# Block inverses on VectorE in pauses, and one wide matmul for state and output, in an RWKV-7 chunk kernel with a routed expert layer

## The chip, the cores and the metric

The kernel runs on one core of one Trainium2 chip. A core has TensorE (matmul), VectorE, ScalarE and GpSimd, each with its own queue of instructions worked off in order, a sync engine that issues most transfers, and 16 DMA engines. In the profile they are called PE (PEld for its weight loads), DVE, ACT, POOL and SP. The metric is the device time of one execution in microseconds. The kernel before takes 809.48 us, the median of three runs from 804.95 to 816.53.

## The reference

Two layers, the first of which takes most of the time.

```python
# RWKV-7: B, H, S, D = 4, 8, 768, 40; all float32
for t in range(S):
    y[:, :, t] = einsum('bhd,bhde->bhe', rt, state)
    Sa = einsum('bhde,bhe->bhd', state, at)
    state = state * wt[:, :, None, :] - einsum('bhd,bhe->bhde', Sa, bt) \
            + einsum('bhd,bhe->bhde', vt, kt)
# experts: x = y as (3072, 320); E = 8, F = 1024, capacity 80
probs = softmax(x @ w_gate); expert = argmax; gate = probs[expert]
# each expert keeps its 80 tokens of the highest gate:
out[tok] = gate[tok] * (relu(x[tok] @ w1[e]) @ w2[e])   # all other rows are 0
```

The recurrence over 768 steps is worked in chunks of T = 64 steps. Within a chunk the values `U` (the corrections that `a` and `b` make) solve a triangular system with a matrix N of 64x64 per head; it is cut into two diagonal blocks of C = 32, whose inverses are computed beforehand, and one block below the diagonal. There are 12 chunks and 2 pairs of batches: 24 units. The state of a pair of batches passes from unit n to unit n + 2.

## The kernel before

A helper `do` keeps the instructions of every engine in the order in which the parts below are called. `copied` transposes a tile on TensorE (`ps_t` holds the result in PSUM) and copies it to SBUF on ScalarE.

```python
AHEAD = NG + 1                       # NG = 4 units share one round of inverses
ps_t = tile_pool("ps_t", bufs=2, space=PSUM)     # transposes and small products
...
def decays(n):      # transpose w, copy on ScalarE to decay
def products(n):    # pt: scan over decay on VectorE
def decayed_a(n):   # transpose a; ahT = -a * pt on VectorE
def inverted(n):    # pp: pt through TensorE; ip = 1 / pp on VectorE;
                    # ub = b * ip and kh = k * ip on GpSimd

def operands(n):
    of[n]["ubT"] = copied("ubT", pairs(of[n]["ub"]), 1)
    of[n]["khT"] = copied("khT", pairs(of[n]["kh"]), 1)

def system(n):      # both triangles: nt[:, 0] = N from ub, nt[:, 1] from kh
    evicted(nt, scores((ubT, khT), ahT))          # 64 matmuls, one copy on ScalarE
    masked(nt, slice(1, 2))                       # on GpSimd
    # the diagonal blocks of N go to DRAM (blocks)

def begin(k):       # lt = blocks from DRAM, one block per partition
    # mask both 16x16 quarters on the diagonal, set the diagonal to 1
def step(k, i):     # i = 1 .. 14, on both quarters (j = 0, 1) together; n = 15 - i
    nc.vector.tensor_tensor(out=tm, in0=t4[:, :, 0:i, i:i+1].to_broadcast([128, 2, i, n]),
        in1=l4[:, :, i:i+1, i+1:].to_broadcast([128, 2, i, n]), op=mult)
    nc.vector.tensor_tensor(out=t4[:, :, 0:i, i+1:], in0=t4[:, :, 0:i, i+1:], in1=tm, op=add)
def end(k):         # inverses to DRAM (solved), a transposed first quarter too (solved_n);
                    # both come back turned, as dt and an
def joint_n(n):     # na = N's lower quarter times the first inverse: 32 matmuls 16x32 x 32
    nc.scalar.copy(na, p)
def joint(n):       # dn = na times the second inverse: 32 matmuls 32x32 x 16
    nc.vector.tensor_tensor(out=o, in0=p, in1=o, op=add)        # into dt
...
def reads_g(n):     # gT: the state turned, 16 matmuls 64x64 x 64, copied by ScalarE
def right(n):       # pr = masked triangle x v, plus ahT x state_b; yy = pr (ScalarE)
def diagonal(n, i): # u = dt[i] x yy; 16 matmuls 32x32 x 40
    nc.vector.tensor_copy(us[n % 2][:, :, 0:D], o["pr"])
def below(n):       # pr += block below the diagonal x u; yy = pr (ScalarE)

def to_state(n):
    for x, y in ((kh, v), (ub, u)):
        for g, q, z in ...:          # 32 matmuls 64x64 x 40
            nc.tensor.matmul(pg[m, z, g, :], lhsT=x[halves[z], 2*g+q, :], rhs=y[halves[z], 2*g+q, 0:D], ...)
    nc.vector.tensor_tensor(out=acc, in0=pg, in1=st[...], op=add)
    nc.gpsimd.tensor_tensor(out=st[...], in0=acc, in1=pt[last step], op=mult)
    load(n + 2, "v")
def spread(n):      # state_b: two copies of the state by ScalarE

def turned(n):      # uT: u transposed
def lower(n):       # lam = scores of vT and uT against rT, one copy, masked on GpSimd
def rows(n):        # yp = gT x rT
def summed(n):
    for x, l in ((kh, lam 0), (ub, lam 1)):
        for g, q, z in ...:          # 32 matmuls 64x64 x 64
            nc.tensor.matmul(y[m, z, g, :], lhsT=x[halves[z], 2*g+q, :], rhs=lam[halves[z], i, q, g, :], ...)
    # xT = yp * pt on VectorE
def logits(n):      # xp = xT through TensorE; rows to DRAM; logit reduction on VectorE
def gate(ci):       # for 4 units: probabilities, weights (exp on ScalarE between),
                    # candidates (og transposed to gp on TensorE), then 10 x eight (max8, match_replace)
...
for n in range(NU + 1):              # a slot: unit n, the output of o = n - 1, the system of m = n + AHEAD
    operands(m); spread(o)
    # n % 4 == 1: probabilities, weights, candidates; n % 4 == 3: steps 5..14 and end; else: eights
    rows(o); system(m); reads_g(n); right(n); inverted(m + 1); turned(o); diagonal(n, 0)
    lower(o); reads(n, r); reads(n, v); below(n); joint_n(n + 1); decays(m + 2)
    decayed_a(m + 1); diagonal(n, 1); joint(n + 1)
    # n % 4 == 2: begin
    summed(o); to_state(n); products(m + 2)
    # n % 4 == 2: steps 1..4
    logits(o)
```

Before the loop the units 0 to NG are prepared, and the first inverse is computed there. After it come the choice of the 80 tokens of each expert and the experts themselves.

Of the kernel before, what the change touches and what calls it, by code (L numbers as in the profile page):

```python
# [18 lines left out]
def kernel(  # L19
# [116 lines left out]
    with ExitStack() as p1:  # L136

        AHEAD = NG + 1
# [4 lines left out]
        ps_t = p1.enter_context(tc.tile_pool(name="ps_t", bufs=2, space=PSUM))  # L143
# [30 lines left out]
        Q = C // 2  # L174
        QS = Q * C + Q
        (inv_t,) = padded("inv_t", 1, [128, 2 * QS])
        (inv_n,) = padded("inv_n", 1, [128, Q, C])

# [36 lines left out]
        def scores(lhs, rhs):  # L215

            p = ps_s.tile([128, 2, 2, G, T], F32, name="sp", tag="s")
            for i in range(2):
                for g in range(G):
                    for z in halves:  # L220
                        for q, m in enumerate(pars):
                            nc.tensor.matmul(p[z, q, i, g, :], lhsT=lhs[i][m, g, z], rhs=rhs[m, g, z],  # L222
                                             start=True, stop=True)
            return p

        def evicted(o, p):
            nc.scalar.copy(o.rearrange("p i q g t -> p q i (g t)"), p.rearrange("p q i g t -> p q i (g t)"))  # L227

        def masked(o, i):

            for z in halves:
                oo = o[z, i].rearrange("p i q g t -> p (i q g) t")
# [8 lines left out]
        solved_n = nc.dram_tensor("solved_n", (NCI, Z, NS, NG, H, Q * C), F32, kind="Internal")  # L241
# [36 lines left out]
        def operands(n):  # L278
            of[n]["ubT"] = copied("ubT", pairs(of[n]["ub"]), 1)
            of[n]["khT"] = copied("khT", pairs(of[n]["kh"]), 1)  # L280

        def system(n):
            o = of[n]
            o["nt"] = nt = kept.tile([128, 2, 2, G, T], F32, name="nt", tag="nt", bufs=AHEAD + 1)
            evicted(nt, scores((o.pop("ubT"), o.pop("khT")), o["ahT"]))
            masked(nt, slice(1, 2))

            for z in range(Z):
                for i in range(NS):
                    nc.sync.dma_start(blocks[n // NG, z, i, n % NG].rearrange("h (s t) -> s h t", s=C),  # L290
                                      nt[block(z, i), 0].rearrange("p q g t -> p (q g) t")[:, :, i * C : (i + 1) * C])


        def quarters(t):
            return t.rearrange("p (j x) -> p j x", j=2)[:, :, 0 : Q * C].rearrange("p j (s t) -> p j s t", t=C)[:, :, :, 0:Q]

        def fetch(k):
            inverse[k]["lt"] = lt = sb.tile([128, 2 * QS], F32, name="lt", tag="lt", bufs=1)
            nc.sync.dma_start(lt[:, 0 : C * C], blocks[k].rearrange("z i u h x -> (z i u h) x"))

        def begin(k):
            for j in range(2):
                nc.gpsimd.affine_select(out=quarters(inv_t)[:, j], in_=quarters(inverse[k]["lt"])[:, j],
                                        compare_op=Alu.is_gt, fill=0.0, base=0,
                                        pattern=[[-1, Q], [1, Q]], channel_multiplier=0)
            nc.gpsimd.memset(inv_t[:, 0 : C * C : C + 1], 1.0)

        def step(k, i):
            l4, t4 = quarters(inverse[k]["lt"]), quarters(inv_t)
            n = Q - 1 - i  # L310
            tmp = sb.tile([128, Q * Q // 2], F32, name="tmp", tag="tmp", bufs=1)
            tm = tmp[:, 0 : 2 * i * n].rearrange("p (j s t) -> p j s t", j=2, s=i)
            nc.vector.tensor_tensor(
                out=tm, in0=t4[:, :, 0:i, i : i + 1].to_broadcast([128, 2, i, n]),
                in1=l4[:, :, i : i + 1, i + 1 :].to_broadcast([128, 2, i, n]), op=Alu.mult)
            nc.vector.tensor_tensor(out=t4[:, :, 0:i, i + 1 :], in0=t4[:, :, 0:i, i + 1 :], in1=tm, op=Alu.add)
# [548 lines left out]
```

## Time and profile before

| | before |
|---|---|
| median of 3 runs | 809.48 us |
| profiled run, and its span | 807.08 us, 805.3 us |
| mean granted TensorE clock | 0.795 of full speed |
| instructions in the span | 34,678 |
| DMA | 73.00 MB, mean 91 GB/s |
| longest single operations on VectorE: reciprocal, scan | 2,156 ns, 1,232 ns |
| VectorE copies of U | 48, 469 ns each |
| GpSimd masks of `lam` and `nt` | 1,140 ns and 690 ns each |

A line of a group gives the source line, the engine and operation, the tiles (output <- inputs), the shape and the count; after a bar the busy time in us and the mean of one in ns; after another bar the idle time of the engine just before these operations and what ended most of it. A line in order of time begins with the start in us and the duration; square brackets hold the idle time before it and its releaser. "issue" is time in which an engine waited for nothing that the profile shows. One float32 matmul of the source shows as two records (and two weight loads), so the 32 joint matmuls of a unit are 64 records and 24 units give 1,536; a transpose shows as one.

### The profile page before, as it was taken

The page shows a single profiled execution, that of the slowest core. Times are in us where ns is not written, and L with a number is a line of the kernel's source. Part 1 is how long each engine was busy: PE and PEld are TensorE (multiplying, and loading weights), DVE is VectorE, ACT ScalarE, POOL GpSimd, SP SyncE. Part 2 cuts the span into 40 slices and gives each one's busy share as a digit, 9 for nine tenths or more (in the row PEclk, how much of TensorE's full clock was granted, in tenths as well). Part 3 has the DMA queues.
Part 4 walks back from the last instruction along what each step waited for, and adds up shares of the span by engine and source line. Part 5 has one row for each costly group of instructions (what it writes and reads, how often), then busy time and mean ns, then how long its engine had stood idle before and what let it go on. Part 6 is the DMA issues. An engine that isn't in the chain of part 4 may idle for free. (4 is left out here: it accounts for less than half of the span.)

```text
span 805.3 us, 34678 instructions
## 1 busy us (share of the span) xinstructions
PE 601.7 (75%) x15974; PEld 526.9 (65%) x15974; DVE 292.4 (36%) x730; ACT 208.4 (26%) x386; POOL 197.4 (25%) x278
## 2 busy tenths in 40 slices
PE   4750789778786787876989869897878860559997
PEld 3540678667676676765878758787768750458775
DVE  7434223613256242561435624334223218500000
ACT  1320234223442144421444213332213210000010
POOL 4530133222332233321333223322011210020101
PEclk9965787859899797976989768886778865566999
DMA  6556733574245742547323461123411004998000
GB/s 107 93 89 112 76 63 72 131 91 89 56 92 144 91 96 59 112 95 90 57 51 70 117 86 34 31 63 76 52 29 30 13 22 154 353 329 256 17 11 16
DMA packets 238469, 73.00 MB, mean 91 GB/s; under 512 B 218100, under 2 KB 232564, under 8 KB 238324
## 3 DMA queue, kind: packets, MB, share of 16 engines
q1 hardware_dynamic: 227680, 64.06, 40.2%
q10 hardware_dynamic: 9876, 4.93, 2.2%
q8 instruction: 125, 2.05, 1.1%
q0 software_dynamic: 768, 1.80, 0.8%
q14 instruction: 20, 0.16, 0.1%
HBM read 53.42 MB, written 17.33 MB: 88 GB/s over the span
## 5 line engine op out<-in xcount | busy, mean ns | idle before, releaser
L272 DVE RECIPROCAL ip<-pp 128x320 f32<-128x320 f32 x24 | 51.8, 2156 | 75.9 <-PE pp L269 75.6
L421 POOL TENSOR_TENSOR state<-acc,pt 128x320 f32<-128x320 f32 x22 | 30.0, 1363 | 164.4 <-DVE acc L420 142.2
L233 POOL TENSOR_SCALAR_AFFINE_SELECT lam<-lam 64x1024 f32<-64x1024 f32 x48 | 54.7, 1140 | 54.4 <-ACT lam L227 52.8
L233 POOL TENSOR_SCALAR_AFFINE_SELECT nt<-nt 64x512 f32<-64x512 f32 x48 | 33.1, 690 | 141.1 <-ACT nt L227 139.5
L342 PE MATMUL na<-an,nt 16*32 16x32 f32 x1536 | 25.3, 205 | 47.1 <-DMA an<-solved_n 46.8
L342 PEld LDWEIGHTS na<-an,nt 16*32 16x32 f32 x1536 | 20.2, 115 | 50.8 <-issue 25.1
L260 DVE SCALAR_TENSOR_TENSOR ahT<-tp,pt 128x512 f32<-128x512 f32 x24 | 16.6, 691 | 92.6 <-PE tp L205 92.0
L404 PE MATMUL pr<-yy,dt 32*32 32x40 f32 x1536 | 40.3, 206 | 4.5 <-ACT yy L389 2.6
L404 PEld LDWEIGHTS pr<-yy,dt 32*32 32x32 f32 x1536 | 33.8, 113 | 13.7 <-issue 7.7
L406 DVE COPY u<-pr 128x320 f32<-128x320 f32 x48 | 22.5, 469 | 52.0 <-PE pr L404 51.1
L450 PE MATMUL yp<-rT,gT 64*64 64x64 f32 x768 | 41.2, 286 | 0.0
L274 POOL TENSOR_TENSOR ub<-raw_b,ip 128x320 f32<-128x320 f32 x24 | 21.6, 898 | 80.0 <-issue 38.2
L450 PEld LDWEIGHTS yp<-rT,gT 64*64 64x64 f32 x768 | 37.1, 194 | 5.7 <-issue 5.5
L821 PE MATMUL yp<-w,hT 128*80 128x320 f32 x128 | 38.6, 450 | 0.0
L815 ACT ACTIVATE hT<-hp 128x320 f32<-128x320 f32 x16 | 6.1, 435 | 125.0 <-PE hp L811 125.0
L256 DVE TENSOR_TENSOR_SCAN pt<-decay,begins 128x520 f32<-128x520 f32 x24 | 29.6, 1232 | 22.8 <-ACT decay L250 22.7
L804 PEld LDWEIGHTS hp<-xe,w 128*128 128x128 f32 x256 | 36.1, 227 | 1.4 <-DVE xe L796 1.3
L804 PE MATMUL hp<-xe,w 128*128 128x80 f32 x256 | 36.3, 311 | 0.0
L463 DVE TENSOR_TENSOR xT<-yp,pt 128x512 f32<-128x512 f32 x24 | 16.6, 691 | 48.9 <-PE yp L459 48.9
L227 ACT COPY nt<-sp 128x1024 f32<-128x1024 f32 x24 | 24.3, 1011 | 35.9 <-PE sp L222 35.8
L823 DVE TENSOR_SCALAR y<-yp,weight 80x320 f32<-80x320 f32 x8 | 4.4, 547 | 77.5 <-PE yp L821 77.5
L227 ACT COPY lam<-sp 128x1024 f32<-128x1024 f32 x24 | 24.3, 1013 | 30.6 <-PE sp L222 30.6
(353 smaller groups left out, 1329.1 us busy)
## 6 DMA issues: line engine op xcount, KB each, us to landing
w<-in_moe_w_dram SPq DMA_DIRECT2D x8, 1280.0 KB, 14.3
w<-in_moe_w_dram SPq DMA_DIRECT2D x8, 1024.0 KB, 15.7
x_rows<-xb SPq DMA_DIRECT2D x48, 96.0 KB, 2.2
out_dram<-zero ACTq DMA_DIRECT2D x8, 480.0 KB, 3.3
raw_w<-in_w_dram SPq DMA_DIRECT2D x46, 80.0 KB, 3.3
raw_a<-in_a_dram SPq DMA_DIRECT2D x46, 80.0 KB, 3.2
raw_b<-in_b_dram SPq DMA_DIRECT2D x46, 80.0 KB, 2.9
raw_k<-in_k_dram SPq DMA_DIRECT2D x46, 80.0 KB, 3.0
```

The lines of the kernel that those rows point to most:

```text
L227: nc.scalar.copy(o.rearrange("p i q g t -> p q i (g t)"), p.rearrange("p q i g t -> p q i (g t)"))
L233: nc.gpsimd.affine_select(out=oo, in_=oo, compare_op=Alu.is_gt, fill=0.0, base=0, pattern=[[0, oo.shape[1]], [1, T]], channel_multiplier=-1)
L256: nc.vector.tensor_tensor_scan(flat(pt), flat(decay[n % 2]), flat(begins), 0.0, op0=Alu.mult, op1=Alu.add)
L272: nc.vector.reciprocal(ip, p.rearrange("p g (q d) -> p (g q) d", q=2))
L274: nc.gpsimd.tensor_tensor(out=ub[:, :, 0:D], in0=raw["b"][n % 2][:, :, 0:D], in1=ip, op=Alu.mult)
L342: nc.tensor.matmul(p[m, h, :], lhsT=nt[mq, 0, h % 2, h // 2, i * C : (i + 1) * C], rhs=an[mq, n % NG, h % 2, h // 2, :], start=h == 0, sto ...
L404: nc.tensor.matmul(o["pr"][m, h, :], lhsT=dt_[m, n % NG, h % 2, h // 2, :], rhs=o["yy"][m, h, :], start=h == 0, stop=True, skip_group_chec ...
L406: nc.vector.tensor_copy(us[n % 2][:, :, 0:D], o["pr"])
L421: nc.gpsimd.tensor_tensor(out=st[:, :, :, 0:D], in0=acc, in1=o["pt"][:, :, :, T : T + 1].rearrange("p g z o -> p z g o").to_broadcast([128 ...
L450: nc.tensor.matmul(y[m, z, g, :], lhsT=o["gT"][m, z, g, :], rhs=o["rT"][m, g, halves[z]], start=g == 0, stop=False, skip_group_check=True)
L804: nc.tensor.matmul(hp[f // (FK // 2)][:, f % (FK // 2), :], lhsT=t1[:, i, f * 128 : (f + 1) * 128], rhs=xe[:, i, :], start=f % (FK // 2) = ...
L821: nc.tensor.matmul(yp, lhsT=hT[:, f, :], rhs=w2[:, f, :], start=f == 0, stop=f == FK - 1)
```

## The change

Three things are done, and the order of the loop is laid out anew around them.

The inverse of a 32x32 block is computed wholly on VectorE: 30 steps over the whole block instead of 14 over two quarters. The two products that joined the quarters on TensorE, their copies and transfers (`an`, `solved_n`, `na`, `dn`) are gone. The steps are put on a list together with the parts of the gate, and `pause(us)` takes as many from the list as fit an assumed time; there are four pauses in a slot, of 5, 1.6, 2.4 and 1.6 us. A step is assumed to take 0.8 us. An inverse begins when its four units are ready and spreads over three slots; units are prepared two slots earlier than before (`AHEAD = NG + 3`).

The products for the state and for the output have the same stationary operands, `kh` and `ub`. They become one: the moving operand `lam` gets 40 more columns with v and U, so that a matmul has 64 + 40 = 104. The state is updated with the output, a slot later than before.

U is copied out of PSUM by ScalarE, not VectorE.

```diff
-        AHEAD = NG + 1
+        AHEAD = NG + 3
-        ps_t = p1.enter_context(tc.tile_pool(name="ps_t", bufs=2, space=PSUM))
+        ps_t = p1.enter_context(tc.tile_pool(name="ps_t", bufs=3, space=PSUM))
...
+        (lam,) = [hold.tile([128, 2, 2, G, T + D], F32, name="lam")]
...
         def step(k, i):
-            l4, t4 = quarters(inverse[k]["lt"]), quarters(inv_t)
-            n = Q - 1 - i
+            n = C - 1 - i
...
             nc.vector.tensor_tensor(
-                out=tm, in0=t4[:, :, 0:i, i : i + 1].to_broadcast([128, 2, i, n]),
-                in1=l4[:, :, i : i + 1, i + 1 :].to_broadcast([128, 2, i, n]), op=Alu.mult)
-            nc.vector.tensor_tensor(out=t4[:, :, 0:i, i + 1 :], in0=t4[:, :, 0:i, i + 1 :], in1=tm, op=Alu.add)
+                out=tm, in0=t3[:, 0:i, i : i + 1].to_broadcast([128, i, n]),
+                in1=l3[:, i : i + 1, i + 1 :].to_broadcast([128, i, n]), op=Alu.mult)
+            nc.vector.tensor_tensor(out=t3[:, 0:i, i + 1 :], in0=t3[:, 0:i, i + 1 :], in1=tm, op=Alu.add)
...
-        def joint_n(n):
-        def joint(n):
-        def to_state(n):
...
+        def operand_k(n):                  # khT apart from ubT, one slot before its use
+        def psi(n):                        # its triangle apart from N, own copy and mask
...
-            nc.vector.tensor_copy(us[n % 2][:, :, 0:D], o["pr"])
+            nc.scalar.copy(us[n % 2][:, :, 0:D], o["pr"])
...
+        def beside(n):
+            for i, x in enumerate((raw["v"][n % 2], us[n % 2])):
+                nc.scalar.copy(lam[:, i, :, :, T:].rearrange("p q g d -> p g q d"),
+                               x[:, :, 0:D].rearrange("p (g q) d -> p g q d", q=2))
+            load(n + 2, "v")
...
         def lower(n):
-            evicted(lam, scores((o["vT"], o["uT"]), o["rT"]))
+            p = scores((o["vT"], o["uT"]), o["rT"])
+            for q in range(2):
+                nc.scalar.copy(lam[:, :, q, :, 0:T], p[:, q])
...
         def summed(n):
+            w_ = T if last else T + D
-                            nc.tensor.matmul(o["y"][m, z, g, :], lhsT=x[halves[z], 2 * g + q, :],
-                                             rhs=o["lam"][halves[z], i, q, g, :], ...)
+                            nc.tensor.matmul(o["y"][m, z, g, 0:w_], lhsT=x[halves[z], 2 * g + q, :],
+                                             rhs=lam[halves[z], i, q, g, 0:w_], ...)
...
+            if not last:
+                nc.vector.tensor_tensor(out=acc, in0=o["y"][:, :, :, T:], in1=st[:, :, :, 0:D], op=Alu.add)
+                nc.gpsimd.tensor_tensor(out=st[:, :, :, 0:D], in0=acc, in1=..., op=Alu.mult)
...
+        def pause(us_):
+            while todo and us_ > 0:
+                cost, f = todo.pop(0)
+                do(f)
+                us_ -= cost
+
+        def invert(k):
+            todo.extend((0.4 * 2, lambda i=i: step(k, i)) for i in range(1, C - 1))
+            todo.append((0, lambda: end(k)))
...
+        invert(0)
+        pause(60)                          # the first inverse, before the loop
...
+        for n in range(NU + 2):            # o = n - 1, m = n + AHEAD
+            logits(o - 1); gate parts onto the list when (o - 1) % 4 == 3
+            operand_b(m); beside(o); spread(o - 1); pause(5)
+            rows(o); system(m); reads_g(n); right(n); inverted(m + 1); pause(1.6)
+            turned(o); reads(n, r); diagonal(n, 0); lower(o); below(n); reads(n, v); operand_k(n + 1)
+            decays(m + 2); decayed_a(m + 1); diagonal(n, 1); pause(2.4)
+            psi(n + 1); begin and invert when m % 4 == 3; summed(o); products(m + 2); pause(1.6)
```

The last block is shortened to the order of the calls. The eight writes of zeros to the output are issued by the sync engine instead of ScalarE.

## The prediction

> **What bounds the kernel now.** I read first the page's shares and its row of slices, then the groups of TensorE by form, then the order of time in some slots (a slot is one pass of the main loop: one chunk of 64 steps for one pair of batches), and last a table of short stretches with the granted clock.
>
> TensorE is the busiest engine, but not full:
>
> ```profile
> PE 601.7 (75%) x15974; PEld 526.9 (65%) x15974; DVE 292.4 (36%) x730; ACT 208.4 (26%) x386; POOL 197.4 (25%) x278
> ```
>
> The copies of gT, one per slot, date the loop: the first starts at 90.87 us, the 24th at 636.43 us. So 23 slots take 545.6 us, 23.7 us each; 91 us lie before and 169 us (routing and experts, which the change leaves alone) after. Between 131.7 and 332.9 us the slots take 26.2, 26.1, 28.5, 20.9, 26.5, 25.5, 26.7 and 20.9 us: a pattern of four. The good one (212.5 to 233.4) has TensorE busy for about 17.15 us at full clock; the rest of it is waits. The groups that the change touches (columns: busy us, mean ns, then idle time before them by releaser):
>
> ```profile
> L342 PE MATMUL na<-an,nt 16*32 16x32 f32 x1536 | 25.3, 205 | 47.1 <-DMA an<-solved_n 46.8 <-issue 0.3
> L353 PE MATMUL dn<-dt,na 32*32 32x16 f32 x1536 | 24.1, 189 | 10.2 <-issue 9.8 <-ACT na L345 0.5
> L416 PE MATMUL pr<-u,ub 64*64 64x40 f32 x704 | 22.4, 262 | 10.7 <-issue 10.7
> L416 PE MATMUL pr<-raw_v,kh 64*64 64x40 f32 x704 | 21.2, 263 | 11.8 <-issue 11.7
> L520 PE MATMUL gp<-ident,og 128*128 128x128 f32 x6 | 2.5, 424 | 20.4 <-DVE og L513 20.4
> ```
>
> Three kinds of idle time show. "issue" stops of about 2 us fall in the middle of a run of equal matmuls, so no operand is missing:
>
> ```profile
> 223.93 0.30 PE L416 MATMUL pr<-u,ub 64*64 64x40 f32 x7
> 226.48 0.56 PE L416 MATMUL pr<-u,ub 64*64 64x40 f32 x25 [2.25 <-issue]
> ```
>
> Real waits come in some slots: for the array `an` from DRAM (about 5 us in every fourth slot), for the gate's `og` (3 to 4.5 us in every fourth), and 2.5 to 3 us for VectorE's logit reduction where inverse steps stand ahead of it. And a wait is paid twice, because the clock falls (columns: stretch, length, busy of PE, PEld, DVE, ACT, POOL; then clock, DMA share, GB/s):
>
> ```profile
> 160.00:164.00 4.00, 2.89 (x106) 2.48 (x102) 0.65 (x2) 2.32 (x4) 3.49 (x4) 1.00 0.78 119
> 164.00:168.00 4.00, 0.61 (x5) 0.32 (x5) 0.00 (x0) 0.00 (x0) 0.48 (x1) 0.55 1.42 101
> 168.00:172.00 4.00, 4.00 (x108) 3.61 (x111) 0.69 (x1) 0.96 (x2) 0.00 (x0) 0.50 0.59 99
> ...
> 176.00:180.00 4.00, 4.00 (x38) 3.63 (x31) 1.83 (x3) 0.43 (x1) 2.17 (x3) 0.50 0.28 46
> 180.00:184.00 4.00, 4.00 (x140) 3.67 (x140) 0.00 (x0) 2.75 (x5) 0.00 (x0) 0.82 0.57 176
> ```
>
> [...] here recovery took some 14 us of full work (to about 181 us)[...]. [...] The page's queue q8 has 125 transfers and 2.05 MB; 31,948 PE instructions over 125 give 256 each, so these are TensorE's, and I read the issue stops as late blocks. [...] the state product on GpSimd takes 0.74 us at 614.11 with VectorE still, but 1.59 us beside a scan, and an inverse step of 28 elements takes 0.65 us instead of 0.19 us behind it:
>
> ```profile
> 249.05 1.59 POOL L421 TENSOR_TENSOR state<-acc,pt 128x320 f32<-128x320 f32 x1 [2.58 <-DVE acc L420]
> 250.03 0.65 DVE L313 TENSOR_TENSOR tmp<-inv_t,lt 128x28 f32<-128x28 f32 x1
> ```
>
> [...] For N = 28 and 112 [...] the trace has 0.19 and 0.27 us. [...]
>
> **The change, part by part.** The two products that join the inverses of the half blocks go. At full clock, in the good slot, the first takes 0.68 us (218.63 to 219.31), the second 0.94 us (220.90 to 222.51 without its 0.67 us stop). The state product (1.28 us: 223.44 to 226.97 without its 2.25 us stop) merges into the output product, whose columns grow from 64 to 104. Those 32 matmuls take 0.46 us; in proportion of the columns 0.75, and at the rate of the other 64x64 product (`gT`, 16 rounds of 64 columns in 1.0 us, so 8 rounds of 104 in about 0.82) a little more. Twice 0.36 us is added. TensorE: -0.68 -0.94 -1.28 +0.72 = -2.2 us per slot, 52 us in all.
>
> TensorE's instructions per slot fall by 128 + 128 + 128 of some 1,310, all from the densest stretch. The issue stops sum to 10 + 11 + 22 = 43 us (the joint's, the output's and the state's), 1.8 us per slot; I keep 0.5 and gain 1.3.
>
> The waits for `an` go: 47 us less 21 before the loop (17.8 + 1.4 + 1.6 and small ones), so 26 us over five slots, and the slow clock behind them. The waits for the logit reduction (8 us) go too, with logits ahead of the steps and a third bank for transposes.
>
> Added: the logits now follow the output product at once, without the state product as cover, so TensorE waits for xT: 0.8 us in the rows where it does so already, say 0.9 per slot.
>
> VectorE: an inverse was 28 operations, 1,120 elements per kind of step: [...] with gaps of 0.035 us 7.7, as the first one shows (60.12 to 67.84). It becomes 60 operations with 4,960 elements[...]. Six of them add 79 us of busy time (85 with the gaps); the U copies (22.5 us) and the joint's addition (7.0 us) leave. What VectorE does in every slot without them: reciprocal 2.16, scan 1.23, xT 0.69, ahT 0.69, acc 0.49, reduction 0.17 = 5.4 us. The pauses put 14 steps each into two slots out of four, 10.9 and 10.1 us: VectorE has 16.3 and 15.5 us there. GpSimd has about 6.9 us per slot that read SBUF (1.74 + 2.34 + 1.38 + 0.74 + 0.24 + 0.45); I let 3 us of it fall onto the steps: 19.3 and 18.5 us. There VectorE, not TensorE, sets the slot.
>
> ScalarE gains two U copies (0.45 us each), two copies into the wide operand (about 0.5 each) and one more scores copy: some 8.5 us become 10.7, under the slot.
>
> **The new slots.** A plain one: 17.15 - 2.2 + 0.9 + 0.5 + 0.35 of small waits = 16.7 us. Two with steps: 19.3 and 18.5. The one with the gate: `og` still comes by way of the exponential on ScalarE, behind four copies and the state's spread, while TensorE has only one transpose to do first: 16.7 + 4 + 3.5 for 8 us of slow clock = 24.2. Mean 19.7; with 0.7 for slow clock elsewhere 20.4 us. The last seven slots lack one transpose, the system scores, the inverted decays and two more transposes (2.6 us): 14.1 x 7 = 99, and 15 for two gates, 4 for the last inverse's steps, 7 for slow clock = 125 us.
>
> Before the loop each unit loses a transpose and half its scores, but two more units are prepared, and the inverse takes 22 us instead of 8 with a stop of TensorE behind it: I estimate steps from about 50 to 72 us, then the trip through DRAM and four scans and reciprocals, and the first gT at about 84 us, against 90.9.
>
> Sum: 84 + 16 x 20.4 + 125 + 169 = 704 us of span, 3 for the first slots in slow clock, and 2 to 3 from span to timed run (807.08 us for a span of 805.3): 710 us.
>
> **Rivals.** First, VectorE becomes the bound everywhere: [...] TensorE waits for the output product's operand, loses its clock and needs 23 us per slot. For it: two thirds of the slots have little slack. Against: there are no steps in one slot of four, and VectorE sat at 36%. That gives 16 x 23 + 140 + 86 + 171 = 765 us. Second, the longer state loop binds: the state is now updated one slot later, after U's transpose, the lower scores, their masks and the wide product, and is read about 4 us into the next slot. Working it out, acc and the state product are ready 3 to 3.5 us after that product, just in time; 1 us of lateness per slot would cost 24 us, 735 in all. Third, the stops for instructions stay or move into other matmuls because the DMA queues are as full as before: +1.3 x 24 = 31 us, 740. Fourth, all is hidden and the clock stays whole except at gates: steps meet little of GpSimd, mean slot 18.5, 675 us.
>
> **Range and chances.** The rivals that cost stand at 735 to 765 and rarely all together; the one that gains at 675. 672 to 755 should hold the time 8 times in 10. No rival brings it back to 793, the edge of 2%: faster 0.95, same 0.03, slower 0.02.
>
> **What would show it.** Right: gT copies 17 to 20 us apart, except one slot in four with a gap before `gp`; no rows for na and dn; TensorE at about 11,500 matmuls; "issue" idle under 20 us; the wide product near 0.83 us for 32 matmuls; xT in front of the logits by about 0.9 us; VectorE near 340 us busy; clock above 0.8 in the loop. Wrong: VectorE idle less than 1 us in slots with steps and TensorE waiting for ahT or xT by more than 2 us; `lam` masks longer than 1.2 us with the wide product waiting; a first gT after 95 us.

## The result, and the profile after

| | before | after |
|---|---|---|
| median of 4 runs each, on one chip | 809.31 us | 672.68 us |
| lowest to highest | 804.95 to 816.53 | 669.64 to 677.32 |
| ratio, 95% interval | | 0.831, 0.823 to 0.839 |
| span of the profiled run, mean granted clock | 805.3 us, 0.795 | 667.9 us, 0.912 |

The predicted 710 us was 37 us too high; the time is at the lower end of the predicted range, 672 to 755 us. The copies of gT divide both spans in the same way, and so do the terms of the prediction's sum (us):

| stage | before | predicted | after | after less predicted |
|---|---|---|---|---|
| up to the first gT | 90.9 | 84 | 106.2 | +22 |
| 16 slots with all parts | 395.9 | 326 | 299.1 | -27 |
| 7 light slots | 149.6 | 125 | 110.6 | -14 |
| after the 24th gT | 168.9 | 169 | 152.1 | -17 |
| span | 805.3 | 704 | 667.9 | -36 |

That the time lies inside the range, by less than 1 us, is luck: the first stage went wrong the other way, and without its 22 us the time would have fallen below the range. The first row of the page after, engines and their busy time:

```profile
PE 500.3 (75%) x11494; PEld 434.3 (65%) x11494; DVE 368.1 (55%) x851; ACT 239.0 (36%) x500; POOL 197.3 (30%) x273
```

TensorE is busy for 101 us less, and its share is again 75%: three quarters of the gain are busy time, one quarter is waiting. VectorE has 76 us more. The groups that answer to those of before (by form; busy us, mean ns, then idle time before them by releaser):

```profile
L417 PE MATMUL yp<-lam,kh 64*64 64x104 f32 x704 | 27.0, 260 | 12.3 <-POOL lam L227 12.1
L417 PE MATMUL yp<-lam,ub 64*64 64x104 f32 x704 | 23.2, 255 | 0.0
L262 PE MATMUL pp<-pick,pt 128*64 128x80 f32 x384 | 22.3, 271 | 29.0 <-DVE pt L249 29.0
L485 PE MATMUL gp<-ident,og 128*128 128x128 f32 x6 | 2.7, 448 | 21.5 <-DVE og L478 21.5
```

The na and dn groups are gone, and so is every "issue" stop of note: they come to 0.4 us in the whole run, from 44.7. The gate's wait is much the same (20.4 us before, 21.5 now). The waits in front of `pp` grew from 10.8 to 29.0 us (20.4 of them in one wait before the loop), and those for the mask of `lam` on GpSimd from 3.3 to 16.2 us. A plain slot, in order of time:

```profile
264.41 0.90 PE L417 MATMUL yp<-lam,kh 64*64 64x104 f32 x32
...
265.13 0.89 PE L417 MATMUL yp<-lam,ub 64*64 64x104 f32 x32
266.09 0.69 DVE L421 TENSOR_TENSOR xT<-yp,pt 128x512 f32<-128x512 f32 x1 [2.08 <-PE yp L417]
...
266.83 1.12 PE L437 MATMUL xp__3910<-pick,xT 128*128 128x88 f32 x8 [0.81 <-DVE xT L421]
```

The two wide products run into each other without a stop, 0.72 us from start to start, and the wait for xT that the prediction set at 0.9 is 0.81 here. The gate's slot is still the bad one; the table of stretches there (length, busy of PE, PEld, DVE, ACT, POOL; then clock, DMA share, GB/s):

```profile
232.00:236.00 4.00, 0.64 (x5) 0.45 (x7) 2.91 (x16) 2.07 (x6) 0.88 (x4) 0.59 0.63 191
236.00:240.00 4.00, 4.00 (x104) 4.00 (x102) 3.39 (x13) 0.59 (x1) 0.00 (x0) 0.55 0.60 177
```

TensorE has 0.64 us of work in the first 4 us, while it waits for og, and does the next 4 at about half clock; VectorE is busy for 2.91 and 3.39 of each.

### The profile page after: what moved, and what is told of

Its sections match the earlier page's. It is cut to its first block, busy times and chain, and to the rows that moved or that the text cites. A ratio compares the mean times of both kernels' runs of the same rounds, so it can differ in the third digit from the quotient of the medians.

```text
span 667.9 us, 25885 instructions
## 1 busy us (share of the span) xinstructions
PE 500.3 (75%) x11494; PEld 434.3 (65%) x11494; DVE 368.1 (55%) x851; ACT 239.0 (36%) x500; POOL 197.3 (30%) x273
## 5 line engine op out<-in xcount | busy, mean ns | idle before, releaser
L303 DVE TENSOR_TENSOR tmp<-tt,lt 128x30 f32<-128x30 f32 (+9 forms) x180 | 75.5, 420 | 25.3 <-POOL tt L292 20.5
L306 DVE TENSOR_TENSOR tt<-tt,tmp 128x30 f32<-128x30 f32 (+9 forms) x180 | 79.3, 441 | 6.6
L267 POOL TENSOR_TENSOR ub<-raw_b,ip 128x320 f32<-128x320 f32 x24 | 21.5, 894 | 200.3 <-DVE ip L265 179.6
L249 DVE TENSOR_TENSOR_SCAN pt<-decay,begins 128x520 f32<-128x520 f32 x24 | 30.0, 1248 | 26.5 <-ACT decay L243 26.5
L262 PE MATMUL pp<-pick,pt 128*64 128x80 f32 x384 | 22.3, 271 | 29.0 <-DVE pt L249 29.0
L417 PE MATMUL yp<-lam,kh 64*64 64x104 f32 (+1 forms) x768 | 29.6, 261 | 16.5 <-POOL lam L227 16.2
L262 PEld LDWEIGHTS pp<-pick,pt 128*64 128x64 f32 x384 | 18.9, 166 | 32.1 <-issue 26.2
L227 POOL TENSOR_SCALAR_AFFINE_SELECT psi<-psi 64x512 f32<-64x512 f32 x48 | 32.2, 672 | 20.2 <-ACT psi L324 18.6
L406 PE MATMUL yp<-rT,gT 64*64 64x64 f32 x768 | 35.9, 260 | 0.0
L417 PEld LDWEIGHTS yp<-lam,kh 64*64 64x64 f32 x768 | 22.0, 140 | 21.2 <-POOL lam L227 21.2
L207 ACT COPY ubT<-tp 128x512 f32<-128x512 f32 x24 | 14.1, 586 | 58.1 <-PE tp L202 58.0
L395 ACT COPY lam<-sp 128x512 f32<-128x512 f32 x48 | 25.8, 589 | 16.8 <-PE sp L220 16.8
```

Source lines behind the costliest of these rows:

```text
L227: nc.gpsimd.affine_select(out=oo, in_=oo, compare_op=Alu.is_gt, fill=0.0, base=0, pattern=[[0, oo.shape[1]], [1, T]], channel_multiplier=-1)
L249: nc.vector.tensor_tensor_scan(flat(pt), flat(decay[n % 2]), flat(begins), 0.0, op0=Alu.mult, op1=Alu.add)
L262: nc.tensor.matmul(p[halves[z], g, :], lhsT=pt[:, g, z, 1:], rhs=pick[:, 0, 0 : 2 * D], start=g == 0, stop=True, skip_group_check=True)
L303: nc.vector.tensor_tensor(out=tm, in0=t3[:, 0:i, i : i + 1].to_broadcast([128, i, n]), in1=l3[:, i : i + 1, i + 1 :].to_broadcast([128, i, ...
L306: nc.vector.tensor_tensor(out=t3[:, 0:i, i + 1 :], in0=t3[:, 0:i, i + 1 :], in1=tm, op=Alu.add)
L395: nc.scalar.copy(lam[:, :, q, :, 0:T], p[:, q])
```

## The experiments

Each is timed against the kernel before, on the chip of its own group of runs. "After" below stands for the changed kernel's 672.7 us. It was not timed again in these groups, in which the median of before was 805.1 to 811.6 us, and its own four runs spread over 7.7 us; so a difference from after of less than some 8 us, or one where the intervals of the ratio overlap with after's 0.823 to 0.839, stays open. The runs of `e3`, `e6`, `e9` and `e10` fall into two groups about 10 us apart, and the lower group is compared with after (the profiled runs of `e3` and `e9` belong to it, with tails of 152 us behind the 24th gT; those of `e6` and `e10` to the other, with 163 and 164 us).

### The joining products alone

`e5_before_no_joint`: the kernel before without the joining products, which leaves out one quarter of each inverse; everything else of the change is absent.

```diff
-        do(joint_n, 0)
-        do(joint, 0)
...
-            inverse[k]["an"] = an = sb.tile([128, NG, 2, G, C], F32, name="an", tag="an", bufs=1)
-                    nc.sync.dma_start(an[p.start : p.start + Q]..., solved_n[k, z, i]...)
...
-                do(joint_n, n + 1)
-                do(joint, n + 1)
```

> The kernel before, with the two products that join the half inverses left out (and the transfer to `an` with them), so that the off-diagonal quarter of the inverse is missing from what is computed. All else stays: the inverses of the halves, the separate state product, U on VectorE. Theory A (the removed products, their instruction stops and the waits for `an` are about half of what the change gained): 38 us of matmuls, 10 us of stops in front of dn, 26 us of waits for `an` in the loop and some slow clock after them, so 725 to 745 us. Rival B (the TensorE work is hidden behind the other waits, and only the waits for `an` were on the path): 775 to 785 us. The groups na and dn are gone; the stops in front of the state product (22 us before) stay under A, since the queue has only 10% fewer instructions.

Measured: 671.14 us (669.48 to 671.81), ratio 0.838 (0.830 to 0.846), 134 us less than its 805.12 of before. That is as much as the whole change gains, and about twice what theory A expected. The engines' row of this kernel's page:

```profile
PE 521.5 (78%) x12902; PEld 451.4 (67%) x12902; DVE 287.0 (43%) x706; ACT 197.2 (29%) x356; POOL 196.1 (29%) x278
```

And three of TensorE's waits there (total in us, times, longest):

```profile
PE gp L515 <- DVE og L508: 20.9, 6, 4.4
PE tp L205 <- DVE lg L471: 11.8, 15, 3.8
...
PE pr L411 <- issue: 7.3, 8, 2.0
```

TensorE is busy for 80.2 us less (601.7 to 521.5), of which the two groups themselves were 49.4. The other 31 us are other matmuls that now run at a better clock (0.871 against 0.795 over the span): the output product with gT, for one, went from 286 to 258 ns a matmul. The waits for `an` (46.8 us) are gone, and the issue stops fell from 44.7 to 10.7 us, although the separate state product, where theory A left 22 us of them, is still there and now shows 7.3. (TensorE lost 19% of its matmuls here, not the 10% of its instructions that the expectation reckoned with.) Against that stand 25 us by which other waits grew (for ub, ip, lg and lam). So -80 - 47 - 34 + 25 = -136, the change of the span.

The stages show what the rest of the change did, net of all (us):

| | before | joint left out | after |
|---|---|---|---|
| up to the first gT | 90.9 | 79.7 | 106.2 |
| gT 1 to 24 | 545.5 | 418.9 | 409.6 |
| after the 24th gT | 168.9 | 170.5 | 152.1 |

Ahead of the loop the full inverse on VectorE, together with the two more units that are prepared there, costs 26.5 us (`e9` below parts the two to some extent); in the loop its cost is more than covered by the other parts (9 us less); and the tail got 18 us shorter.

### The U copy

`e4_u_on_vector`: after, with U copied by VectorE again. `e11_before_u_on_scalar`: before, with U copied by ScalarE, the same line the other way.

```diff
-            nc.scalar.copy(us[n % 2][:, :, 0:D], o["pr"])
+            nc.vector.tensor_copy(us[n % 2][:, :, 0:D], o["pr"])
```

> The changed kernel with U copied out of PSUM by VectorE again. Theory: VectorE stands in a pause full of steps when U is needed, so the first copy of U (before the block below the diagonal) waits up to 2 us behind steps in two slots of four, and the second up to 3; the product below the diagonal waits for it on TensorE. Expect 685 to 700 us, with TensorE idle before the product below and VectorE's two U copies 22 us busy. Rival: VectorE has room, 673 to 678 us.

> The kernel before, with U copied by ScalarE instead of VectorE, and nothing else. Theory A (the copy matters only where long inverse steps stand ahead of it on VectorE, and before the change none did: no wait for U shows in its trace): 803 to 813 us, no difference. Rival B (relief of VectorE is worth something by itself): 770 to 795 us, with shorter waits for the logit reduction and for og.

Measured: 738.86 us (733.97 to 740.9), ratio 0.913 (0.906 to 0.920), so +66 us in after; and 804.64 us, ratio 0.997 (0.994 to 1.000), in before, so nothing that can be told from zero. The copy itself is as long on either engine (0.48 and 0.43 us). The order of time of `e4_u_on_vector` (VectorE and the lower product that needs U) shows where it goes:

```profile
237.40 2.15 DVE L265 RECIPROCAL ip<-pp 128x320 f32<-128x320 f32 x1
...
239.77 0.91 DVE L306 TENSOR_TENSOR tt<-tt,tmp 128x168 f32<-128x168 f32 x1
...
241.60 1.13 DVE L306 TENSOR_TENSOR tt<-tt,tmp 128x150 f32<-128x150 f32 x1
242.65 0.48 DVE L373 COPY u<-pr 128x320 f32<-128x320 f32 x1
...
243.18 1.27 PE L362 MATMUL pr<-u,nt 32*32 32x40 f32 x32 [6.29 <-DVE u L373]
```

U stands in VectorE's order behind the steps and the reciprocal; TensorE waits 6.29 us and then takes 1.27 us for what it does in 0.76. Fourteen such waits come to 55.2 us. The theory had only a part of that. The part that looks smallest in the diff is the one without which half of the gain would be lost.

### The wide product

`e3_split_product`: after, with the product of 104 columns taken apart into 64 and 40.

```diff
-                                              rhs=lam[halves[z], i, q, g, 0:w_], ...
+                                              rhs=lam[halves[z], i, q, g, 0:T], ...
+            for i, x in enumerate((o["kh"], o["ub"])):
+                (the same four loops, with columns T:w_)
```

> The changed kernel with its wide product taken apart on TensorE only: 32 matmuls of 64 columns and then 32 of 40 columns per slot, with the same operands and everything else unchanged; that adds 64 records of matmuls and 64 weight loads per slot. Theory A (TensorE's own work): +0.5 us per slot, 685 us, with no issue stops. Theory B (instruction supply): the stops of about 2 us come back near these matmuls, 0.5 to 1.5 us per slot more, 695 to 715 us, and the idle time put down to issue grows from 0 to over 10 us. Theory C (slots are set by VectorE and the gate): under 5 us.

Measured: 684.81 us (678.16 to 696.59), without an interval. The lower two runs, 678.16 and 678.55 us, are 6 us longer than after; the loop of the profiled one is 10.8 us longer (420.4 us against 409.6). So theory A's 0.5 us per slot is right in size, but in the whole time it cannot be told from theory C's "under 5 us". Busy time of the products grows from 54.8 us (27.0 + 23.2, and 4.6 for the last two units, which have no state product) to 78.6 us (22.1 + 19.6 + 18.6 + 18.3), TensorE's whole busy time by 12.4 us, and the issue stops grow from 0.4 to 7.1 us, 4.2 of them in front of the new matmuls. They do not come back to the 22 us that stood in front of the state product before; so it is not this product alone that makes them.

### The steps and GpSimd

`e6_no_steps`: after without the inverse's steps in the five later rounds. `e7_masks_without_reading`: after with GpSimd's masks of the scores as fills, so that these scores are zero.

```diff
-            todo.extend((0.4 * 2, lambda i=i: step(k, i)) for i in range(1, C - 1))
+            todo.extend((0.4 * 2, lambda i=i: step(k, i)) for i in range(1, C - 1 if k == 0 else 1))
```

```diff
-                nc.gpsimd.affine_select(out=oo, in_=oo, compare_op=Alu.is_gt, fill=0.0, base=0,
-                                        pattern=[[0, oo.shape[1]], [1, T]], channel_multiplier=-1)
+                nc.gpsimd.memset(oo, 0.0)
```

> The changed kernel, with the inverse's steps left out in the five later rounds (the first inverse is still worked out in full, the later ones stay what the masks leave); transfers, masks and all products stay. Theory A (the steps set the length of the slots that carry them): the two slots out of four with steps fall from about 20 us to 15.7, so ten slots times 4 us and two shorter ones: 630 to 645 us, lam waits from 16 to under 6 us. Rival B (TensorE and the gate set the slots, the steps lie in VectorE's pauses): within 8 us of the changed kernel, 665 to 672 us.

> The changed kernel, with GpSimd's masks of the scores replaced by fills with zero of the same size: they write the same tiles and wait for the same copies, but read nothing (so the lower scores are zero in what is computed). Theory A (a step on VectorE that falls beside a GpSimd operation reading SBUF is held up): the steps' mean falls from 0.42 to 0.44 us to at most 0.37 us, no step over 0.7 us beside a fill, and the time falls by 8 to 20 us, to 652 to 664 us. Rival B (the length of the steps comes from their own operands): the mean stays at 0.42 to 0.44 us; the time changes only by what a fill is shorter than a mask, under 6 us.

Measured: 638.44 us (635.02 to 647.66, the lower group to 638.51) without the steps, some 35 us less than after, ratio 0.795 (0.788 to 0.803); the loop is 33.0 us shorter and the waits for `lam` fell from 16.2 to 5.5 us, although the waits for `og` grew from 21.5 to 30.7 us (10.9 of them in one new wait). With fills 660.21 us (654.93 to 662.25), 12.5 us less, and 7.4 us less in the loop; but the ratio, 0.822 (0.813 to 0.831), overlaps with that of after, so the gain in time is likely and not shown.

Theory A holds in both, in the second for the length of the steps (mean 0.376 us, close to the 0.37 it named). The first inverse, which has GpSimd to itself and is the only one left in `e6_no_steps`, takes 10.0 + 10.0 us there for its 60 operations (332 ns each). The six inverses of after take 75.5 + 79.3 = 154.8 us (420 and 441 ns); with fills 67.5 + 67.7 = 135.2. Here is a step of 220 elements in one slot of after, in order of time (start, duration), VectorE and GpSimd only:

```profile
203.00 0.86 POOL L267 TENSOR_TENSOR ub<-raw_b,ip 128x320 f32<-128x320 f32 x1 [7.19 <-DVE ip L265]
203.18 0.91 DVE L306 TENSOR_TENSOR tt<-tt,tmp 128x210 f32<-128x210 f32 x1
...
204.78 2.53 POOL L227 TENSOR_SCALAR_AFFINE_SELECT lam<-lam 64x1024 f32<-64x1024 f32 x2
205.10 1.20 DVE L306 TENSOR_TENSOR tt<-tt,tmp 128x220 f32<-128x220 f32 x1
```

The same step of the same slot with fills:

```profile
203.20 1.94 POOL L227 MEMSET lam<- 64x1024 f32 x2
203.54 0.39 DVE L305 TENSOR_TENSOR tt<-tt,tmp 128x220 f32<-128x220 f32 x1
```

The step of 220 elements beside the mask takes 1.20 us, beside the fill 0.39. Beside the products ub and kh, which read SBUF in both kernels, a step is as long as before (0.91 and 0.94 us). A mask reads its tile, a fill does not: in these traces a step is long beside the GpSimd operations that read (0.91 to 1.20 us), and not beside the one that only writes (0.39 us). The slots with steps went from 19.4, 20.0 and 19.9 us to 17.3, 16.9 and 16.8, the gate's slots of 23.4 us did not get shorter (23.6, 23.8 and 23.2). A fill is also shorter than a mask (0.95 against 1.17 us, two in a slot), but 0.4 us does not make 2 to 3.

### The tail

`e1_late_sl`: after with one tile, which the diff moved from a pool of its stage to the pool of constants, put back. `e2_before_late_const`: before with that tile in the constants, and nothing else.

```diff
-        late = const.tile([128, 256], BF16, name="late")
+        late = sl.tile([128, 256], BF16, name="late")
```

> The changed kernel with one line set back: the small tile `late`, which feeds the 48 matmuls that keep TensorE at work between routing and experts, lies in the routing's pool again and not among the constants. Theory: that line alone made the end shorter. The gathered rows take the place of the routing's tiles, so the first gather waits for the last of the 48 matmuls; TensorE then idles some 7 us and does the first experts at half clock. Expect about 688 us, a gap of 7 to 8 us before the first transposed rows, and the first two experts' products of 32 matmuls at 6 to 7 us instead of 3.7. Rival: the end is shorter because the weights of the experts arrive sooner or the clock happened to stay; then 673 us and no gap.

> The kernel before with that one line alone: `late` among the constants. Theory: the end shortens by the same 15 to 17 us, 793 us, and the first gather no longer waits for the still matmuls. Rival (the end of the changed kernel is shorter for reasons of its loop): 809 us.

Measured: 688.44 us (687.25 to 691.49), ratio 0.853 (0.846 to 0.859), +15.8 us on after, on the mark of the 688 us expected. In before the same line gave 802.41 us, ratio 0.990 (0.986 to 0.994): 7 to 9 us, half of what was expected. TensorE in order of time at the start of the experts, in after:

```profile
579.09 7.94 PE L133 MATMUL still_p<-late 128*128 128x256 bf16 x48
587.32 0.40 PE L764 MATMUL xp<-ident,rows 80*128 80x80 f32 x3 [0.30 <-DMA rows<-x_rows,idx_g]
...
589.02 3.74 PE L774 MATMUL hp<-xe,w 128*128 128x80 f32 x32
```

The same in `e1_late_sl`:

```profile
596.76 0.63 PE L764 MATMUL xp<-ident,rows 80*128 80x80 f32 x3 [7.56 <-DMA rows<-x_rows,idx_g]
...
598.44 7.04 PE L774 MATMUL hp<-xe,w 128*128 128x80 f32 x32
```

The 48 matmuls on `late` have one purpose, to keep TensorE at work while the first rows are gathered. With the tile in the stage's own pool the gather starts only when they are over: the wait is 7.56 us, the clock falls (to 0.5 in the slice of the page from 601.9 to 619.1 us), and two experts' products take 7.04 us instead of 3.74. In before the line did remove the late gather (the wait fell from 7.74 to 2.43 us), but in the profiled run of `e2_before_late_const` the products still took 7.04 us, as at half clock in `e1_late_sl`. That run took 812.53 us, the longest of thirteen; the shortest took 794.72, and whether the clock stayed whole there is not shown. More on the clock at the end.

### The order of work

Four kernels in which no operation is added or left out.

`e8_gate_one_pause_later` hands out the transposes of the gate's candidates one pause later:

```diff
-            return [(1.1, probabilities), (1.1, weights_of), (0.3, candidates)] + [
+            return [(1.1, probabilities), (5, weights_of), (0.3, candidates)] + [
```

> The changed kernel, with the weight given to the gate's second part raised from 1.1 to 5, so that the transposes of the gate's candidates are handed out one pause later, when VectorE has og ready; nothing else moves. Theory A (a wait is paid twice, by itself and by the slow clock behind it): the waits in front of gp fall from 21.5 us to under 8, and five gate slots get 4 to 6 us shorter: 640 to 650 us. Rival B (only the wait itself counts, or the work that moves meets another wait): 655 to 668 us.

Measured: 651.24 us (648.76 to 656.55), ratio 0.815 (0.806 to 0.825), 21 us less than after and just above theory A's 640 to 650 us. The two ratios differ by only 13 us and their intervals just touch; the traces have the loop 19.4 us shorter (390.2 us against 409.6). The waits in front of `gp` fell from 21.5 to 3.0 us. The gate's slots of 23.4, 23.4 and 23.4 us became 17.8, 19.9 and 17.7, the two light ones of 19.9 and 19.3 became 14.8 and 15.0. The wait of the first of these slots in after, and then its whole stretch in this kernel:

```profile
235.36 0.45 PE L485 MATMUL gp<-ident,og 128*128 128x128 f32 x1 [3.77 <-DVE og L478]
```

```profile
215.30:233.10 17.80, 15.45 (x474) 13.94 (x471) 16.87 (x37) 9.65 (x22) 7.77 (x10) 1.00 0.45 87
```

The clock stays at 1.00 (0.85 over this slot in after), and a wait of 3.77 us was worth 5.6. The next slot but one gave 3 back (15.9 to 19.1).

`e9_prologue_pipelined` prepares units 4 to 7 as units 0 to 3 are prepared, and hands out the first inverse's steps between them, six at a time in the trace (the expectation says four). `e10_begin_a_slot_later` starts each later inverse at the top of the next slot.

```diff
-        for n in range(NG, NG + 2):
+        for n in range(NG, NG + 4):
...
-        pause(60)
-        for n in range(NG + 2, NG + 4):
+                do(operand_b, n - 1)
+                do(system, n - 1)
+                pause(4)
```

```diff
+            if 0 < n and m <= NU and m % NG == 0:
+                do(begin, m // NG - 1)
+                invert(m // NG - 1)
             if o >= 1:
                 do(logits, o - 1)
...
-            if coming and m % NG == NG - 1:
-                do(begin, m // NG)
-                invert(m // NG)
```

> The changed kernel, with units 4 to 7 prepared as units 0 to 3 are (the lower half of one unit is worked on beside the upper half of the next), and the first inverse's steps handed out four at a time between them instead of all in one pause. Theory A (the serial preparation and the one stop of 20.4 us before the loop are lost time): the first gT at 84 to 90 us instead of 106, the wait of 20.4 us in front of pp is gone, and the whole run is 14 to 22 us shorter: 651 to 659 us. Rival B (the loads or VectorE set the length before the loop): the first gT stays after 98 us, under 8 us gained.

> The changed kernel, with the copy that opens each later inverse (tt, on GpSimd) and its steps put at the top of the next slot, so that GpSimd does not stand before it for lt, with the state product behind it. Theory A (GpSimd's order of work makes a late transfer into a late state): the 7.3 us in front of gp__2556 and the 1.4 us in front of gp__6767 go, and the slot that took 23.3 us takes 16; 8 to 12 us shorter with its slow clock: 660 to 665 us. Rival B (the steps start later, and dt comes too late for the next group of four): waits in front of pr for dt, 672 to 685 us.

Measured for the first: 663.5 us (658.06 to 668.42), without an interval; the lower two runs, 658.06 and 658.95 us, are 14 us less than after, within theory A's 651 to 659. But it came about in another way. The first gT came at 84.2 us as expected, but the slot after it took 26.3 us instead of 11.2. TensorE in that slot:

```profile
93.87 1.34 PE L262 MATMUL pp<-pick,pt 128*64 128x80 f32 x16 [7.44 <-DVE pt L249]
...
99.43 1.27 PE L371 MATMUL pr<-yy,dt 32*32 32x40 f32 x30 [1.11 <-DMA dt<-solved]
```

The steps, spread so thinly, ended at 92.4 us instead of 83.8, and the first system needed them: the stop had moved, and 6 of the 22 us were left at the fifth gT (167.7 against 174.0). Another 5 us of the profiled run come from one slot (18.5 us against 23.3) in which TensorE waited 2.4 us for a late state instead of the 7.3 us shown next.

For the second: 671.92 us (664.59 to 678.21), ratio 0.824 (0.817 to 0.832). The lower two runs, 664.59 and 668.29 us, are 4 to 8 us less than after, which its spread does not tell from zero. The wait that it was made for is gone. In after it was a chain over three engines (start, duration, idle before):

```profile
193.08 1.27 POOL L292 TENSOR_SCALAR_AFFINE_SELECT tt<-lt 128x1024 f32<-128x1024 f32 x1 [8.33 <-issue]
194.48 0.73 POOL L427 TENSOR_TENSOR state<-acc,pt 128x320 f32<-128x320 f32 x1
195.27 1.97 PE L338 MATMUL gp__2556<-ident,state 64*64 64x64 f32 x32 [7.25 <-POOL state L427]
```

The slot with it fell from 23.3 to 15.3 us. But the steps came later, and met the gate: its slots went from 23.4 to 24.9, 26.1 and 26.4 us. Neither theory had it so. All slots together gained 3.5 us in the loop (409.6 to 406.1).

`e12_together` has all of these, with eleven steps at a time before the loop (the expectation says ten), and the transposes of ub ahead of the logits:

```diff
+            if coming:
+                do(operand_b, m)
             if o >= 1:
                 do(logits, o - 1)
```

> The changed kernel with four moves of order together: units 4 to 7 prepared in a pipeline, now with ten of the first inverse's thirty steps at a time between them (four were too slow, the last came only at 92 us); the gate's candidates a pause later; the opening of each later inverse at the top of the next slot; and the transposes of the next unit's B ahead of the logits, as work for TensorE while it waits for xT. No operation is added or dropped. Theory A (each wait removed is worth its own length, less some overlap): 24 us for the gate, 10 to 16 before the loop, up to 12 for xT (0.8 to 2.0 us in 24 slots, of which the transposes cover 0.7), 4 for begin: 615 to 635 us; waits for xT under 5 us in all, first gT at 86 to 92 us. Rival B (VectorE's steps and GpSimd's order of work are the limit of the heavy slots, and waits only change their name): 640 to 650 us, no better than the gate's move alone, with lam waits above 20 us.

Measured: 647.19 us (643.2 to 648.43), ratio 0.806 (0.796 to 0.816). Better than both kernels, and some 4 us below the gate's move alone, with intervals that overlap; rival B had 640 to 650. TensorE's waits in this kernel (total, times, longest):

```profile
PE pp L262 <- DVE pt L249: 30.1, 8, 9.0
PE yp L417 <- POOL lam L227: 17.9, 22, 3.9
...
PE gp L485 <- DVE og L478: 4.0, 4, 3.0
```

The gate's wait is gone, the waits for xT fell from 27.4 to 17.3 us in all (theory A said under 5), and those for `pp` and `lam` are as long as ever. The first gT comes at 93.4 us, the next one 20.6 later. The loop takes 389.9 us, against 390.2 with the gate's move alone. So in the loop waits did change their names, as rival B said, though it expected more of them at `lam`. The 12 us that the first gT came earlier than with the gate's move alone (93.4 against 105.5) were gained, but this profiled run has a tail of 162.7 us in place of 152.4, which takes 10 of them back. Without steps (`e6_no_steps`) the loop takes 376.6.

## Why the prediction was right, and where it was not

**The joining products and their waits: right in kind, too small.** The prediction charged 1.62 us of matmuls per slot (39 us in all), 1.3 us of issue stops per slot (31), and 26 for `an`, some 96 us. Taken out alone they gave 134. The missing terms are the clock of the other matmuls (31 us) and the waits for `an` before the loop, which it set aside (21 of 47); against them stand the 25 us by which other waits grew. The stops had been put at 1.3 us gained of 1.8; all 44.7 us went. Rival 3, that they would stay, fell: after has 0.4 us of them, and the other kernels with as many matmuls have up to 4.6.

**The wide product: right.** Predicted 0.82 us for 32 matmuls, measured 0.72, so in proportion of the columns (0.75). The wait for xT, predicted 0.9 per slot, is 27.4 / 24 = 1.14. The prediction's own terms (1.28 us for the state product, less 2 x 0.36 us for the added columns) make 13 us in 24 slots; the split gave back 6 us of the time and 10.8 us of the loop.

**The slots: right in size, wrong in order.** Predicted 16.7, 19.3, 18.5 and 24.2 us in turn (78.7 for four). Four slots of after, from 197.3 us on, take 19.4, 23.4, 15.7 and 15.9 (74.4). The step that failed is the count: the gate's work waits in the same list behind the steps, so the gate's slot and the second one with steps are the same slot, and two slots are plain. VectorE is busy for 21.0 of that slot's 23.4 us. The plain ones are also 0.8 to 1.0 us better than worked out, with no stop at all where 0.5 were charged.

**VectorE: the mechanism right, the total low.** The first inverse takes 22.0 us with its gaps, as predicted (22, the author's estimate). An estimate from the trace of before alone comes to the same: a line through its mean steps of 52 elements (213 ns) and of 112 (274 ns) gives 19.7 us for the 60 operations, 4,960 elements of each kind, and 21.8 with gaps of 0.035 us. Busy time was to be near 340 us and is 368: the 20.0 us of the first inverse hold only where GpSimd is still, and the later five take (154.8 - 20.0) / 5 = 27.0. The prediction had allowed for that in its slots (3 us in each of two), so the slots came out well, and only its own sign for VectorE was set without it. Rival 1, VectorE as the bound, holds in the slots with steps (18.6 us busy of 19.4 in one) and nowhere else; all later steps cost some 35 us.

**The U copies: not valued.** They stood in the sum as 22.5 us leaving VectorE and two copies more on ScalarE. Left on VectorE they would have cost 66 us, as TensorE waits for them at once. The prediction missed nothing in the total through this, since it took the move as given, but it gave no reason for it.

**Before the loop: wrong.** The failing step is "I estimate steps from about 50 to 72 us, then the trip through DRAM and four scans and reciprocals, and the first gT at about 84 us". The steps took the expected 22 us but from 61.8 to 83.8, and TensorE has no work ahead of it meanwhile:

```profile
85.06 1.33 PE L262 MATMUL pp<-pick,pt 128*64 128x80 f32 x16 [20.42 <-DVE pt L249]
```

Then units 6 and 7 are prepared one after the other, 11 us each from scan to scan (83.7 to 94.7), none beside another. This was one of the prediction's own signs of being wrong, and it came: 106 against 95 us.

**The tail: wrong.** "169 us (routing and experts, which the change leaves alone)" overlooked one line of the diff, the pool of `late`. It is worth 15.8 us in after.

**Rival 2, the longer state loop,** did not bind: TensorE's waits for the state come to some 9 us, 7.3 of them in the one slot where GpSimd stood in front of `lt`. **Rival 4** named the right time, 675 us, for a reason that fell: not all is hidden, some 35 us of steps and 20 of gate are on the path.

## What to carry to other kernels

When a part with many small matmuls is taken out, value it by a run that leaves it out, not by the sum of its rows: here the rows gave 96 us and the run 134, since the clock and the stops of everything else improved. An engine that is to take long new work in its pauses must first lose every short operation on which another engine waits at once: the same U copy was worth nothing before and 66 us after. And read a diff for the pools and the order of its lists as well as for its operations; a tile's pool was worth 16 us, and a number in a list some 20.

## What was not expected of the hardware

**The clock of the first two experts goes with one stretch of 3.4 us in front of them.** After the 48 filling matmuls come six transposes of gathered rows, with waits, and then the first product of 32 matmuls. In some kernels this product took 3.74 us, in others 6.6 to 7.04 us at half clock, and there the tail of the changed kernel is 9 to 12 us longer. No single wait decides it: after has one of 1.03 us before the second rows and `e3` one of 1.42 us, and both kept the clock. The start of the experts in `e12_together`:

```profile
547.46 6.79 PE L133 MATMUL still_p<-late 128*128 128x256 bf16 x48
556.17 0.40 PE L759 MATMUL xp<-ident,rows 80*128 80x80 f32 x3 [1.92 <-DMA rows<-x_rows,idx_g]
...
557.79 7.03 PE L769 MATMUL hp<-xe,w 128*128 128x80 f32 x32
```

In all of these kernels TensorE ran at half clock (0.50) up to the filling matmuls and came back to full clock (1.00) in the midst of them. When it rose and fell can be worked out from the mean clock of stretches of 1 us (one of 0.83 rose from 0.50 to 1.00 after a third of it), and TensorE's busy time between can then be read off:

| kernels | clock back, after the start of the 48 | busy, second 3.41 us after that | first product |
|---|---|---|---|
| after, `e3`, `e7`, `e8`, `e9` | 5.2 to 5.7 us | 2.3 to 2.9 us | 3.74 us |
| `e2`, `e4`, `e6`, `e10`, `e12` | 2.9 to 3.5 us | 0.8 to 1.4 us | 6.6 to 7.04 us |

In the five kernels of the second row the clock fell 6.82 to 6.84 us after it had come back, which is twice 3.41; in the first row it did not fall. In the traces of before and after, all 84 stretches of one clock that end with a change last 3.41 us or a whole multiple of it (in before, 0.50 from 102.96 to 106.38 us, then 1.00 to 120.03, which is four of them). The last 3.41 us before the fall need not be empty: it came after 1.35 us of work there in `e10`, and did not come after 2.28 us in `e3`. An early return also makes the 48 matmuls shorter (6.8 to 7.1 us against 7.9 to 8.2), while in the changed kernels the first rows come 8.2 to 8.7 us after the start of them, so that the gap grows. No run varied the number of filling matmuls, so this is read from ten traces and not tested by an edit. The way back to full clock took longer than that: in `e12_together` dense products stay at half clock (0.50) for some 18 us (557.8 to 575.7), and the runs do not show why.

**The issue stops are no constant per instruction.** TensorE has 15,974 matmul records and 44.7 us of stops in before; 12,902 and 10.7 without the joint; 11,494 and 0.4 in after. A fifth fewer matmuls took away three quarters of the stops; `e3_split_product`, with 12,902 records too, has 7.1. That late transfers of instructions are behind it is likely: the page's queue `q8 instruction` has 125 transfers in before, 101 in `e3_split_product` and 90 in after, and in the trace of before each of the 29 stops over 0.3 us ends 1.2 to 1.7 us after the end of one. No run tested it apart.
